# Transposing q and k of the later chunks by the DMA crossbar instead of on TensorE, in a retention layer followed by a gated FFN

## The chip, the cores and the metric

The kernel runs on one core of a Trainium2 chip. The metric is the device time of one execution in microseconds (us). A time "before" and a time "after" are medians of several executions on the same chip. The profiled execution's span, which is from the first to the last instruction that the profile shows, is some 1.7 us shorter than its device time (246.4 us for 248.13), so spans are compared with spans and times with times. Ratios are the mean time of one kernel's fast runs over that of the other's of the same rounds, which is not quite the ratio of the medians quoted. A run counts as slow when it is over 1.5% above the fastest of the same kernel; all others are fast.

## The reference

Two layers. The first is a recurrent attention with a decaying state, for 4 batches, 8 heads, 768 positions and head width 64; the second a gated feed-forward net on its 3072 tokens of width 512.

```
state = gamma[h] * state + outer(k[t], v[t])        # per batch and head
y[t]  = q[t] @ state / sqrt(64)
x     = y as (3072, 512)
out   = (sigmoid(x @ w_gate) * (x @ w_val)) @ w_out  # d_ff = 1536
```

## The kernel before

The positions are cut into chunks of 128 (24 chunks over all batches, numbered g), and the tokens into six tiles t of 512. In a chunk the attention is a few small matmuls: scores of k against q, a mask, the product with v, and a term with the state of the chunks before. For these, q and k must be transposed (64 head dimensions on the partitions). TensorE does this, into PSUM, and ScalarE copies the result to SBUF:

```python
def transposes(g):
    tp = pa.tile([128, 2 * NP, C], BF16, tag="tp", name="tp")
    for i, x in enumerate((kn[g], qn[g])):
        for p in range(NP):                                   # NP = 4 pairs of heads
            nc.tensor.transpose(tp[:, i * NP + p, :], pair(x, p), ident)
    qkT[g] = at.tile([128, 2 * NP, C], BF16, tag="qkT", name="qkT", bufs=3)
    nc.scalar.activation(qkT[g], tp, AX.Copy)

def step_t(g):
    transposes(g)
    scale_v(g, nc.vector if g < 8 else nc.gpsimd)

def step_s(g):
    scores(g)
    masks(g)
```

The feed-forward groups of tile t are interleaved with the attention steps of tile t + 1, and the loads of the chunks after that are issued by GpSimd at the start of the tile. Each engine is given its instructions in program order:

```python
def attention(t):            # nine steps for the four chunks of tile t
    g = 4 * t
    return [lambda: step_t(g), lambda: step_s(g), lambda: step_t(g + 1), lambda: step_y(g, g + 1), ...]

for t in range(NT):
    groups = [lambda n1=n1: up(t, n1) for n1 in range(0 if t else 4, NFF)]   # 12 groups of 8 matmuls
    groups += [lambda sm=sm: down(t, sm) for sm in range(4)]                 # 4 groups of 12, each with an output store by SyncE
    steps = attention(t + 1) if t + 1 < NT else []
    if t + 2 < NT:
        for g in range(4 * t + 8, 4 * t + 12):
            load_chunk(g)                                                    # three DMAs issued by GpSimd
    ...                                                                      # a group, then as many steps as are due
```

Of the kernel before, what the change touches and what calls it, by code (L numbers as in the profile page):

```python
# [10 lines left out]
BF16 = mybir.dt.bfloat16  # L11
# [6 lines left out]
def kernel(  # L18
# [10 lines left out]
    nc = tc.nc  # L29
# [3 lines left out]
    C = 128  # L33
    NCH = S // C
    NP = H // 2
# [8 lines left out]
    ld = ctx.enter_context(tc.tile_pool(name="ld", bufs=12))  # L44
# [5 lines left out]

    NG = B * NCH
    NT = N_TOK // 512
    qn, kn, vf = {}, {}, {}

    def src(x, g):
# [3 lines left out]
    def load_v(g, eng):  # L59
        vf[g] = ld.tile([C, H, D], F32, tag="vf", name="vf", bufs=8)  # L60
        eng.dma_start(out=vf[g], in_=src(v, g))  # L61

    def load_kq(g):
        kn[g] = ld.tile([C, H, D], BF16, tag="kn", name="kn")
        qn[g] = ld.tile([C, H, D], BF16, tag="qn", name="qn")
        nc.gpsimd.dma_start(out=kn[g], in_=src(k, g))  # L66
        nc.gpsimd.dma_start(out=qn[g], in_=src(q, g))  # L67

    def load_chunk(g):
        load_kq(g)  # L70
        load_v(g, nc.gpsimd)
# [55 lines left out]
    xT, vs, qkT, sc, stA, stB, y = {}, {}, {}, {}, {}, {}, {}  # L127
    zps = {}

    def pair(t, p):  # L130
        return t[:, 2 * p:2 * p + 2, :].rearrange("s h d -> s (h d)")
# [4 lines that stand above are left out]
            for p in range(NP):  # L136
                nc.tensor.transpose(tp[:, i * NP + p, :], pair(x, p), ident)  # L137
        qkT[g] = at.tile([128, 2 * NP, C], BF16, tag="qkT", name="qkT", bufs=3)
        nc.scalar.activation(qkT[g], tp, AX.Copy)  # L139

    def scale_v(g, eng):
        vs[g] = ld.tile([C, H, D], BF16, tag="vs", name="vs", bufs=4)
        eng.tensor_tensor(vs[g], vf[g], tabv[:, g % NCH, :].unsqueeze(2).to_broadcast([C, H, D]),  # L143
                          op=ALU.mult)
# [52 lines left out]
        nc.vector.tensor_tensor(xT[g // 4][:, :, col:col + C], y[g], taby[:, :, c * C:(c + 1) * C], op=ALU.mult)  # L197

    def step_t(g):
        transposes(g)  # L200
        scale_v(g, nc.vector if g < 8 else nc.gpsimd)

    def step_s(g):
# [14 lines left out]
    def attention(t):  # L218
        g = 4 * t
        return [lambda: step_t(g), lambda: step_s(g), lambda: step_t(g + 1), lambda: step_y(g, g + 1),  # L220
                lambda: step_t(g + 2), lambda: step_y(g + 1, g + 2), lambda: step_t(g + 3),
                lambda: step_y(g + 2, g + 3), lambda: step_y(g + 3)]
# [4 lines left out]
    def up(t, n1, lo=0, hi=512):  # L227
        if t not in hT:
            hT[t] = ffn.tile([128, NFF, 512], BF16, tag="hT", name="hT", bufs=2)
        ps = []  # L230
        for w in (wg, wv):
            u = pf.tile([128, 512], F32, tag="ff", name="ff")
            for kk in range(KT):
                nc.tensor.matmul(u[:, lo:hi], w[:, kk, n1 * 128:(n1 + 1) * 128], xT[t][:, kk, lo:hi],  # L234
                                 start=(kk == 0), stop=(kk == KT - 1))
            ps.append(u)
        gs = ffn.tile([128, 512], F32, tag="gs", name="gs")
        nc.scalar.activation(gs[:, lo:hi], ps[0][:, lo:hi], AX.Sigmoid)  # L238
        nc.vector.tensor_tensor(hT[t][:, n1, lo:hi], gs[:, lo:hi], ps[1][:, lo:hi], op=ALU.mult)  # L239

    def down(t, sm):
        o = pf.tile([128, 512], F32, tag="ff", name="ff")
        for n1 in range(NFF):
            nc.tensor.matmul(o, hT[t][:, n1, sm * 128:(sm + 1) * 128], wo[:, n1, :],  # L244
                             start=(n1 == 0), stop=(n1 == NFF - 1))
        ob = ffn.tile([128, D_MODEL], F32, tag="ob", name="ob")
        nc.scalar.copy(ob, o)  # L247
        row = t * 512 + sm * 128
        nc.sync.dma_start(out=out[row:row + 128, :], in_=ob)
# [23 lines left out]
    transposes(0)  # L273
    keep_on(8)
    scale_v(0, nc.vector)
    scores(0)
    state(0)
# [3 lines left out]
    make_taby(slice(256, 384))  # L281
    transposes(1)
    scale_v(1, nc.vector)
    inter(0)
    intra(0)
# [41 lines left out]

    for t in range(NT):
        groups = [lambda n1=n1: up(t, n1) for n1 in range(0 if t else 4, NFF)]
        groups += [lambda sm=sm: down(t, sm) for sm in range(4)]  # L330
        steps = attention(t + 1) if t + 1 < NT else []
        if t + 2 < NT:
            for g in range(4 * t + 8, 4 * t + 12):
                load_chunk(g)
        first = 0 if t else 6
        done = 0
        for i, group in enumerate(groups):
            group()
            upto = -(-len(steps) * (i + 1 - first) // (len(groups) - first))
            while done < min(upto, len(steps)):  # L340
                steps[done]()
                done += 1
# [30 lines left out]
```

## Time and profile before

| | before |
|---|---|
| time, median of 3 | 248.32 us (248.23 to 248.34) |
| span of the profiled run | 246.4 us |
| TensorE busy | 234.1 us, 95% |
| next engine (ScalarE) | 106.0 us, 43% |
| tile 2 / 3 / 4, first matmul to first matmul | 37.27 / 37.14 / 37.37 us |
| eight transposes of a chunk on TensorE | 0.445 us |

The page cuts the span into 40 slices of 6.2 us; each digit is the busy share of a slice in tenths (9 is 90% or more), and PEclk is the granted clock of TensorE in tenths. PE is TensorE, PEld its weight loads, DVE VectorE, ACT ScalarE, POOL GpSimd, SP SyncE; SPq or ACTq is the issue of a DMA by that engine, and L153 is line 153 of the kernel. From the kernel before:

```profile
PE   7689998997999999999999999999999999999993
...
PEclk9999999999999999999999999999999999999998
DMA  9999999999999932994012100002100002200022
```

From the fourth slice to the last but one TensorE is busy and at full clock, but for two dips before 62 us. The DMA engines are full in the first 14 slices, and full once more in slices 17 and 18, from about 98 to 111 us: these are the last twelve loads. They begin where tile 2 begins.

### The profile page before, as it was taken

What the parts mean: (1) busy time and instruction counts of PE and PEld (TensorE: products, weight loads), DVE (VectorE), ACT (ScalarE), POOL (GpSimd) and SP (SyncE); (2) the same over time, 40 slices, a digit from 0 to 9 for tenths busy, and PEclk for the clock granted to TensorE, in tenths of its full rate; (3) what the DMA queues carried; (4) which work ended last, traced back from release to release, by engine and by line L of the source; (5) the groups of instructions that cost most, each with busy time, mean ns of one, the idle gap of its engine ahead of it and who ended that gap; (6) DMA issues with size and microseconds to landing.
All of it is one profiled execution on the core that took longest, in us unless ns stands there. A gap on an engine that the chain in (4) does not pass through costs nothing.

```text
span 246.4 us, 4449 instructions
## 1 busy us (share of the span) xinstructions
PE 234.1 (95%) x1816; PEld 123.3 (50%) x1816; DVE 101.5 (41%) x168; ACT 106.0 (43%) x191; POOL 91.5 (37%) x111
## 2 busy tenths in 40 slices
PE   7689998997999999999999999999999999999993
PEld 7565644554455554445554445544445554444441
DVE  2565444563446631246631256541256532234300
ACT  7788333425444431454443444342444542233221
POOL 8986574987999912961111001111000000000000
PEclk9999999999999999999999999999999999999998
DMA  9999999999999932994012100002100002200022
GB/s 146 181 198 196 192 213 203 176 208 232 229 174 127 188 80 84 145 180 61 3 41 78 54 3 3 0 17 92 64 0 3 0 0 88 85 0 3 0 85 85
DMA packets 64212, 24.13 MB, mean 98 GB/s; under 512 B 51969, under 2 KB 59649, under 8 KB 64193
## 3 DMA queue, kind: packets, MB, share of 16 engines
q0 software_dynamic: 57616, 16.78, 62.2%
q1 hardware_dynamic: 5536, 6.82, 8.2%
q10 hardware_dynamic: 1040, 0.26, 0.5%
q8 instruction: 14, 0.23, 0.4%
q14 instruction: 6, 0.04, 0.1%
HBM read 28.31 MB, written 6.29 MB: 140 GB/s over the span
## 4 chain that ended last, share of the span: by engine, by line
PE 91%; ACT 7%; issue 1%; DVE 0%; POOL 0%; POOLq 0%; ACTq 0%
PE ff L234 50%; PE ff L244 26%; PE tp L137 4%; PE sA L153 3%; ACT qkT L139 2%; PE y L189 2%; ACT taby L122 2%; PE z L175 2%; PE y L165 2%; PE ff L254 2%; ACT zbd L183 1%; ACT L307 1%; ACT ob L247 0%; ACT gs L238 0%; DVE xT L197 0%
## 5 line engine op out<-in xcount | busy, mean ns | idle before, releaser
L239 DVE TENSOR_TENSOR hT<-gs,ff 128x512 bf16<-128x512 f32 (+2 forms) x76 | 50.1, 660 | 85.6 <-PE ff L234 81.9
L234 PE MATMUL ff<-xT,wg 128*128 128x512 bf16 (+2 forms) x304 | 74.7, 368 | 1.2 <-DVE xT L197 1.1
L234 PE MATMUL ff<-xT,wv 128*128 128x512 bf16 (+2 forms) x304 | 74.6, 368 | 0.0
L238 ACT ACTIVATE gs<-ff 128x512 f32<-128x512 f32 (+2 forms) x76 | 43.6, 573 | 55.4 <-PE ff L234 55.4
L244 PE MATMUL ff<-wo,hT 128*128 128x512 bf16 x288 | 65.0, 379 | 0.0
L234 PEld LDWEIGHTS <-wv 128*128 128x128 bf16 x304 | 29.3, 98 | 33.2
L244 PEld LDWEIGHTS <-hT 128*128 128x128 bf16 x288 | 27.3, 98 | 32.1
L234 PEld LDWEIGHTS <-wg 128*128 128x128 bf16 x304 | 27.4, 98 | 28.4 <-issue 1.4
L143 POOL TENSOR_TENSOR vs<-vf,tabv 128x512 bf16<-128x512 f32 x16 | 16.6, 1058 | 65.0 <-PE y L189 60.1
L247 ACT COPY ob<-ff 128x512 f32<-128x512 f32 x24 | 14.1, 586 | 54.9 <-PE ff L244 50.5
L139 ACT ACTIVATE qkT<-tp 128x1024 bf16<-128x1024 bf16 x24 | 24.6, 1024 | 13.4 <-PE tp L137 13.3
L197 DVE TENSOR_TENSOR xT<-y,taby 128x512 bf16<-128x512 f32 x24 | 16.4, 684 | 20.6 <-PE y L189 20.6
L158 DVE TENSOR_TENSOR stA<-sA,causal 128x512 bf16<-128x512 f32 x24 | 16.5, 687 | 19.9 <-PE sB L153 19.9
L61 POOL DMA_DIRECT2D vf<-in_v_dram x23 | 21.0, 913 | 5.0 <-issue 2.0
L66 POOL DMA_DIRECT2D kn<-in_k_dram x23 | 21.0, 913 | 3.3 <-DMA wo<-in_moe_w_out_dram 1.7
L67 POOL DMA_DIRECT2D qn<-in_q_dram x23 | 20.6, 897 | 2.6 <-DMA wo<-in_moe_w_out_dram 1.7
L183 ACT CAST zbd<-z 64x256 bf16<-64x256 f32 x40 | 14.7, 367 | 12.1 <-PE z L175 11.8
L159 DVE TENSOR_TENSOR stB<-sB,causal 128x512 bf16<-128x512 f32 x24 | 16.3, 680 | 0.0
L153 PE MATMUL sA<-qkT 64*128 64x128 bf16 x96 | 9.5, 219 | 5.5 <-ACT qkT L139 5.4
L153 PEld LDWEIGHTS <-qkT 64*128 64x128 bf16 x192 | 5.4, 94 | 10.6 <-ACT qkT L139 6.8
L254 PE MATMUL ff<-ident 128*128 128x128 bf16 x104 | 9.0, 252 | 1.6 <-POOL ident masks.py:199 1.6
L189 PE MATMUL y<-stA,vs 128*64 128x128 bf16 x96 | 9.9, 222 | 0.0
(36 smaller groups left out, 123.1 us busy)
## 6 DMA issues: line engine op xcount, KB each, us to landing
out_dram<-ob SPq DMA_DIRECT2D x24, 256.0 KB, 2.0
vf<-in_v_dram POOLq DMA_DIRECT2D x23, 256.0 KB, 7.2
kn<-in_k_dram POOLq DMA_DIRECT2D x23, 128.0 KB, 7.2
qn<-in_q_dram POOLq DMA_DIRECT2D x23, 128.0 KB, 7.1
wg<-in_moe_w_gate_dram POOLq DMA_DIRECT2D x6, 256.0 KB, 8.7
wv<-in_moe_w_val_dram POOLq DMA_DIRECT2D x6, 256.0 KB, 9.2
wo<-in_moe_w_out_dram POOLq DMA_DIRECT2D x4, 384.0 KB, 10.7
qf<-in_q_dram ACTq DMA_DIRECT2D x1, 256.0 KB, 4.5
```

Source lines behind the costliest of these rows:

```text
L61: eng.dma_start(out=vf[g], in_=src(v, g))
L66: nc.gpsimd.dma_start(out=kn[g], in_=src(k, g))
L67: nc.gpsimd.dma_start(out=qn[g], in_=src(q, g))
L139: nc.scalar.activation(qkT[g], tp, AX.Copy)
L143: eng.tensor_tensor(vs[g], vf[g], tabv[:, g % NCH, :].unsqueeze(2).to_broadcast([C, H, D]), op=ALU.mult)
L153: nc.tensor.matmul(sc[g][i][:, p, :], t[half, p, :], t[half, NP + p, :], start=True, stop=True)
L158: nc.vector.tensor_tensor(stA[g], sc[g][0], causal4, op=ALU.mult)
L183: nc.scalar.copy(zbd[g % 2][half, :, half], zps[b][half])
L234: nc.tensor.matmul(u[:, lo:hi], w[:, kk, n1 * 128:(n1 + 1) * 128], xT[t][:, kk, lo:hi], start=(kk == 0), stop=(kk == KT - 1))
L238: nc.scalar.activation(gs[:, lo:hi], ps[0][:, lo:hi], AX.Sigmoid)
L239: nc.vector.tensor_tensor(hT[t][:, n1, lo:hi], gs[:, lo:hi], ps[1][:, lo:hi], op=ALU.mult)
L244: nc.tensor.matmul(o, hT[t][:, n1, sm * 128:(sm + 1) * 128], wo[:, n1, :], start=(n1 == 0), stop=(n1 == NFF - 1))
```

## The change

The intent is to take the transposes of chunks 12 to 23 off the bounding engine and leave them to the DMA crossbar, which goes from SBUF to SBUF without PSUM and ScalarE.

```diff
+    XBAR = 12
...
+    def xbar(g):
+        qkT[g] = ld.tile([128, 2 * NP, C], BF16, tag="qkX", name="qkX", bufs=8)
+        for i, x in enumerate((kn[g], qn[g])):
+            nc.sync.dma_start_transpose(out=qkT[g][:, i * NP:(i + 1) * NP, :],
+                                        in_=x.rearrange("s h d -> s (h d)"))
...
     def step_t(g):
-        transposes(g)
+        if g < XBAR:
+            transposes(g)
         scale_v(g, nc.vector if g < 8 else nc.gpsimd)
...
         if t + 2 < NT:
             for g in range(4 * t + 8, 4 * t + 12):
                 load_chunk(g)
+        for g in range(4 * t + 4, 4 * t + 8):
+            if XBAR <= g < NG:
+                xbar(g)
```

## The prediction

> **What bounds the kernel now.** I read first the page's busy shares and its row of granted clock, then the chain of work that ended last in order of time, then the busy times by stretch, with a stretch for each 512-token tile, and last the timeline and the DMA landings around the place where the new transfers start. The page says that TensorE is busy nearly all the span and that nothing else comes near it:
>
> ```profile
> PE 234.1 (95%) x1816; PEld 123.3 (50%) x1816; DVE 101.5 (41%) x168; ACT 106.0 (43%) x191; POOL 91.5 (37%) x111
> ```
>
> Columns are busy us, share and instruction count. Busy time of pipelined matmuls overlaps, so I do not use it as work, only as absence of gaps. The busy times by stretch show where there are none; I cut at the first matmul of tiles 2, 3, 4 and 5, which the chain gives:
>
> ```profile
> 99.65:136.92 37.27, 37.27 (x286) 18.80 (x284) 15.62 (x24) 16.05 (x28) 13.16 (x15) 1.00 0.65 86
> 136.92:174.06 37.14, 37.14 (x278) 18.68 (x276) 15.62 (x24) 15.26 (x26) 4.17 (x4) 1.00 0.08 30
> 174.06:211.43 37.37, 37.37 (x282) 18.99 (x280) 15.64 (x24) 15.37 (x26) 0.00 (x0) 1.00 0.08 29
> ```
>
> After the length come busy us of PE, PEld, DVE, ACT and POOL, then clock, DMA share, GB/s. In the three tiles that the change touches, TensorE is busy for the whole length at full clock. So in this stage an instruction taken off TensorE is worth its start-to-start time, and a wait put on TensorE costs its whole length. ScalarE at 16 of 37 us is far from binding. The chain of waits in order of time (start, length, what) then shows what one tile looks like, here the start of tile 2 and of tile 3:
>
> ```profile
> 99.65 1.73 PE ff L234 x8
> 101.38 0.45 PE tp L137 x8
> 101.82 1.73 PE ff L234 x8
> 103.55 0.16 PE sA L153
> ...
> 136.92 1.73 PE ff L234 x8
> 138.65 0.45 PE tp L137 x8
> 139.09 1.73 PE ff L234 x8
> 140.82 0.16 PE sA L153
> ```
>
> The eight transposes of a chunk take 0.44 to 0.45 us of TensorE's stream, not 8 x 219 ns. And the first scores of a tile, which read the transposed q and k, come only 3.9 us after the tile starts: two "up" groups and one set of transposes. That second fact decides the case. The change is described as one tile ahead, but in program order the transfers of chunks 4t+4 to 4t+7 are issued at the start of tile t, and these chunks' attention steps are run inside tile t. The lead of the first chunk is two groups, not a tile.
>
> **What the Trainium skill says.** "TensorE: Matmul & The Clock Gate", Part 1 (The HAM clock gate), measures 55.6 ns from start to start of warm matmuls with N = 128, and says that an idle window of about 3.4 us can put the clock back to half. The trace agrees with the first (0.445 / 8 = 55.6 ns); no long gap exists in it to show the second. "VectorE: DVE Perf Modes", The three transpose paths, gives 1309 ns for one 128x128 bf16 transpose by the DMA crossbar against 390 ns on TensorE; the trace has no crossbar transpose. "DMA: Bandwidth & Descriptors", Latency and other measured facts, gives a transpose rate of 261 GB/s in one kernel; not in this trace either. The same page, Queues, rings and completion order, says that a DMA engine goes round its queues packet by packet, so that loads issued by GpSimd and transfers issued by SyncE share it. The trace agrees: the same 256 KB output store lands in 2.0 us in quiet and in 4.2 us when loads run (below).
>
> **The change, part by part.**
>
> Removed from TensorE: 12 chunks (12 to 23, four in each of tiles 2, 3, 4) x 0.445 us = 5.34 us, all of it on the path. This is the most that can be won: 248.32 - 5.34 = 243.0, 2.15%.
>
> Removed from ScalarE: 12 evictions of 1024 ns, 12.3 us. None of that is on the path: in these tiles TensorE never waits for one.
>
> Added: 24 transfers of 128 KB, SBUF to SBUF, on SyncE's queue, eight at the start of each of three tiles. SyncE is in order, and the last output store of the tile before stands ahead of them. It waits for the copy of the last "down" result. In the timeline (start, length, what) of tiles 2 and 3:
>
> ```profile
> 100.34 0.33 SPq L249 DMA_DIRECT2D out_dram<-ob  x1
> 137.61 0.33 SPq L249 DMA_DIRECT2D out_dram<-ob  x1
> ```
>
> So the first transpose can be issued at 100.67 and 137.94. With their own transposes gone, the scores are due at 103.55 - 0.44 = 103.1 and 140.82 - 0.44 = 140.4. Both k and q must land in 2.4 us, behind a 256 KB store on the same queue. Tile 4 is the same (store at 174.76, scores due at 177.5).
>
> Quiet tiles (3 and 4). The store issued at 137.61 lands 2.0 us later, at 139.6; I take 0.5 us of this as its acknowledgement, so that its data end near 139.1. Then 256 KB of k and q at 261 GB/s take 1.0 us, and landing another 0.5: 140.6, 0.2 us late. If the rate is half that for transfers this small, or if SyncE needs nearer 1 us than 0.33 us to issue one, it is 1.2 to 1.5 us late. I take 0.8 us for each of the two tiles, an estimate from these two ends.
>
> Tile 2 is not quiet. GpSimd runs ahead: blocked until 97.0 by buffers of the scaled v, it then issues the twelve loads of chunks 20 to 23 from 98.0 to 109, just as the transposes begin. The stretches of DMA and the landings of DMAs issued from 100 to 101 us:
>
> ```profile
> 98.00:113.00 15.00, 15.00 (x109) 7.35 (x108) 6.19 (x10) 6.73 (x11) 11.42 (x14) 1.00 1.49 171
> 113.00:120.00 7.00, 7.00 (x63) 3.75 (x62) 4.33 (x8) 3.54 (x7) 1.29 (x2) 1.00 0.03 6
> 137.60:145.00 7.40, 7.40 (x54) 3.78 (x53) 3.44 (x6) 3.30 (x5) 0.00 (x0) 1.00 0.10 37
> ```
>
> ```profile
> vf<-in_v_dram POOLq DMA_DIRECT2D x1, 256.0 KB, 6.9
> out_dram<-ob SPq DMA_DIRECT2D x1, 256.0 KB, 4.2
> ```
>
> A DMA share over 1 means that the engines hold more than one packet at a time: they are full until 113, then empty. The store ahead of the transposes lands at 104.5, already after the scores are due; data done near 104.0. With half the engines' turns, 256 KB at 130 GB/s take 2.0 us, with landing 106.5: TensorE waits 3.4 us. A wait of this length may also cost a stretch at half clock.
>
> Later chunks of a tile are due 7 to 25 us after the first, and their transfers run meanwhile; even at 3 us apiece they come in time in a quiet tile. Buffers don't bind: eight destination buffers hold two tiles of chunks, and a chunk's buffer is read last two tiles before it is wanted again.
>
> Sum: 248.32 - 5.34 + 3.4 + 2 x 0.8 = 248.0 us.
>
> **Rivals.**
>
> First, everything is hidden: the crossbar lands k and q in under 2.4 us even behind the store. For it speaks that SBUF to SBUF needs no HBM access and that the store's own data are 1 us of traffic. Against it speaks tile 2, where a plain store already lands too late. With tiles 3 and 4 free and tile 2 at 2.5 us: 245.5. Hidden in all three: 243.0.
>
> Second, the crossbar itself becomes the bound. If one 128x512 transfer cost four times the 1309 ns of one 128x128 (5.2 us, an estimate from the skill's figure), a tile would need 8 x 5.2 = 42 us against 35.4 us of matmul work, each first chunk would be 9 to 10 us late, and later ones too: three tiles would go to over 45 us, about 270 in all. Against it: 1309 ns for 32 KB looks like a latency, and 261 GB/s for a real kernel contradicts it.
>
> Third, the middle with more loss: contention in tile 2 costs 6 us and the gap brings half clock for some us, quiet tiles lose 2 us each: 248.3 - 5.3 + 6 + 2 + 4 = 255.
>
> Fourth, unburdening ScalarE or the PSUM bank of the transposes helps elsewhere. Nothing in the three tiles waits for them, so I give this nothing.
>
> **Range and chances.** The gain is sure to some hundredths of a us and the loss is open, from 2.5 us to some 10 us, most likely about 5. This puts the middle at 248.0 and 8 chances in 10 between 244.5 and 252.5. Faster by over 2% (under 243.35) needs under 0.4 us of waits in all, which tile 2's loads all but exclude: 0.05. Slower by over 2% (over 253.3) needs 10 us of waits: 0.14. Within 2%: 0.81.
>
> **What would show it.** In the changed profile: no transposes after 93 us; tiles 2 to 4 would have 35.4 us of matmuls each, and one gap on TensorE in each, ahead of the first scores, released by the DMA that writes the q and k tile, about 3.4 us in tile 2 and about 0.8 us in tiles 3 and 4. The store ahead of the transposes would land at times like before. Wrong would be: gaps ahead of the second to fourth chunk's scores (then the rate of the crossbar is the matter), no gap at all, a lower granted clock in tile 2 for long, or gaps of equal size in all three tiles (then issue or latency, not the loads, set them).

## More of the kernel before

The page's list of DMA queues (packets, MB, share of 16 engines) will be needed later:

```profile
q0 software_dynamic: 57616, 16.78, 62.2%
q1 hardware_dynamic: 5536, 6.82, 8.2%
```

Queue q0 has the loads that GpSimd issues, q1 what SyncE issues.

## The result, and the profile after

The time after is 256.01 us (255.13 to 256.66, 4 runs) against 248.30 us; the ratio is 1.0309, 95% interval 1.0272 to 1.0345. The change is slower by 3%, outside the predicted range. (Line numbers are shifted by the added lines: the "up" matmuls are at L242, the "down" matmuls at L252, the scores at L160.) The page of the kernel after:

```profile
PE 228.4 (90%) x1694; PEld 118.1 (47%) x1720; DVE 101.6 (40%) x168; ACT 95.1 (38%) x179; POOL 91.6 (36%) x111
...
PE   6679998988999999249999979999979999999993
...
PEclk9999999999999999959999999999999999999999
DMA  9999999999999916999601264002253002200022
```

TensorE lost work as intended, and its row now has three holes, at slices 17 to 18, 24 and 30: the beginnings of tiles 2, 3 and 4. The first hole is deep and wide, and the clock drops in it. The busy DMA stretch of slices 17 to 19 is longer than before. The waits of the kernel after name the cause (who waited, for what: us in total, times, longest):

```profile
PE sA L160 <- DMA qkX<-qn: 10.7, 3, 7.8
```

There are just three waits, one ahead of the first scores of each tile, for the landing of the transposed q. Second to fourth chunks of a tile cause none. The timeline at the starts of tile 2 and tile 3 (start, length, what, idle time before it) shows both sizes:

```profile
100.85 1.36 SPq L145 DMA_TRANSPOSE qkX<-kn  x1
102.31 1.28 SPq L145 DMA_TRANSPOSE qkX<-qn  x1
...
110.98 0.26 PE L160 MATMUL sA<-qkX 64*128 64x128 bf16 x1 [7.80 <-DMA qkX<-qn]
...
145.52 1.23 SPq L145 DMA_TRANSPOSE qkX<-kn  x1
...
146.84 1.22 SPq L145 DMA_TRANSPOSE qkX<-qn  x1
...
149.32 0.21 PE L160 MATMUL sA<-qkX 64*128 64x128 bf16 x1 [1.46 <-DMA qkX<-qn]
```

Tile 2's wait is 7.80 us, tile 3's 1.46 us, and tile 4 has the rest of the 10.7, 1.44 us. In the quiet tile 3 SyncE is occupied for 1.22 us with each transpose (a plain store takes it 0.33 us), and q is there 2.44 us after its own start (landing at 149.28). In tile 2 it is there 8.63 us after its start (landing at 110.94).

The busy times by stretch around tile 2's hole (length, busy us of PE, PEld, DVE, ACT, POOL, then clock, DMA share, GB/s) show what followed the hole:

```profile
103.00:111.00 8.00, 0.20 (x3) 0.12 (x4) 0.69 (x1) 0.00 (x0) 5.73 (x7) 0.75 1.76 159
111.00:113.00 2.00, 2.00 (x12) 0.91 (x12) 1.29 (x2) 0.00 (x0) 0.00 (x0) 0.50 2.24 170
113.00:115.00 2.00, 2.00 (x8) 0.79 (x7) 0.36 (x1) 0.60 (x1) 0.00 (x0) 0.80 1.18 115
115.00:117.00 2.00, 2.00 (x11) 0.91 (x10) 0.96 (x2) 0.60 (x1) 0.00 (x0) 1.00 1.77 66
```

The clock fell to half at 107.0 us, 3.8 us after TensorE ran dry. The matmuls after the hole start at half clock, at 110.98, and are at full clock again from 113.8 us, 2.8 us later.

The balance on spans: 246.4 - 5.34 (transposes gone) + 10.7 (waits) + 1.3 (half clock, measured below) = 253.1, against a span of 253.4 us.

My theory after this comparison had three parts. In tile 2 the transposes share the DMA engines with the twelve loads and are late for that. In the quiet tiles they are late because two transposes cost SyncE 1.3 us each and the lead is 2.4 us. And both are a matter of lead alone, as nothing else suffers. The rivals: tile 2's transposes are slow by themselves, behind the store and each other; each tile pays alike; transposes slow something else too.

### The profile page after: what moved, and what is told of

Read it like the earlier page. It is cut to its first block, busy times and chain, and to the rows that moved or that the text cites. A ratio compares the mean times of both kernels' runs of the same rounds, so it can differ in the third digit from the quotient of the medians.

```text
span 253.4 us, 4271 instructions
## 1 busy us (share of the span) xinstructions
PE 228.4 (90%) x1694; PEld 118.1 (47%) x1720; DVE 101.6 (40%) x168; ACT 95.1 (38%) x179; POOL 91.6 (36%) x111
## 3 DMA queue, kind: packets, MB, share of 16 engines
q1 hardware_dynamic: 18592, 9.97, 17.7%
## 4 chain that ended last, share of the span: by engine, by line
PE 79%; ACT 9%; DMA 7%; issue 2%; SPq 1%; POOL 1%; DVE 0%; ACTq 0%
PE ff L242 45%; PE ff L252 23%; DMA qkX<-qn 5%; PE sA L160 3%; ACT taby L123 3%; ACT qkT L140 2%; PE y L196 2%; PE z L182 2%; PE y L172 2%; PE tp L138 2%; DMA qn<-in_q_dram 1%; ACT ob L255 1%; ACT zbd L190 1%; SPq L145 1%; ACT L315 1%
## 5 line engine op out<-in xcount | busy, mean ns | idle before, releaser
L242 PE MATMUL ff<-xT,wg 128*128 128x512 bf16 (+2 forms) x293 | 74.4, 371 | 1.7 <-DVE xT L204 1.1
L242 PE MATMUL ff<-xT,wv 128*128 128x512 bf16 (+2 forms) x296 | 73.8, 369 | 0.4
L252 PE MATMUL ff<-wo,hT 128*128 128x512 bf16 x281 | 64.3, 379 | 0.5 <-issue 0.2
L242 PEld LDWEIGHTS <-wv 128*128 128x128 bf16 x304 | 29.4, 98 | 33.7 <-issue 1.0
L242 PEld LDWEIGHTS <-wg 128*128 128x128 bf16 x304 | 28.0, 98 | 31.7 <-issue 2.2
L252 PEld LDWEIGHTS <-hT 128*128 128x128 bf16 x288 | 27.3, 98 | 32.1
L160 PE MATMUL sA<-qkX 64*128 64x128 bf16 x48 | 4.9, 224 | 10.7 <-DMA qkX<-qn 10.7
L140 ACT ACTIVATE qkT<-tp 128x1024 bf16<-128x1024 bf16 x12 | 12.3, 1023 | 4.8 <-PE tp L138 4.8
L160 PE MATMUL sA<-qkT 64*128 64x128 bf16 x48 | 4.7, 219 | 5.5 <-ACT qkT L140 5.4
```

Of the source, the lines that this page charges most:

```text
L160: nc.tensor.matmul(sc[g][i][:, p, :], t[half, p, :], t[half, NP + p, :], start=True, stop=True)
L242: nc.tensor.matmul(u[:, lo:hi], w[:, kk, n1 * 128:(n1 + 1) * 128], xT[t][:, kk, lo:hi], start=(kk == 0), stop=(kk == KT - 1))
L252: nc.tensor.matmul(o, hT[t][:, n1, sm * 128:(sm + 1) * 128], wo[:, n1, :], start=(n1 == 0), stop=(n1 == NFF - 1))
```

## The experiments

All results were correct. The diffs are against the changed kernel unless said otherwise.

**Only the quiet tiles.**

```diff
-    XBAR = 12
+    XBAR = 16
```

> Chunks 12 to 15 keep their TensorE transposes; only chunks 16 to 23 go through the crossbar, so only the two quiet tiles (3 and 4) are changed. My theory (each quiet tile gains 4 x 0.445 us and loses one wait of 1.46 us, the loss is tile 2's loads): 248.3 - 3.56 + 2.92 = 247.7 us, no drop of the granted clock. Rival (every tile pays alike, a third of the 7.7 us lost): 253.4 us.

Measured: 248.14 us (247.90 to 248.38), before 248.25, ratio 0.9995 (0.9980 to 1.0010). The waits:

```profile
PE sA L160 <- DMA qkX<-qn: 3.0, 2, 1.6
```

Two waits of 1.5 us each, as in the changed kernel's quiet tiles, and hardly any gain is left: a quiet tile wins 1.78 us and loses 1.5. The rival, that every tile pays alike, is out. The time is some 0.4 us above the expectation, which the interval nearly covers; the traces show most of it before anything was changed, as the first scores of tile 2 come at 103.89 us here and at 103.55 in the kernel before.

**The loads moved away from tile 2's transposes.**

```diff
             for g in range(4 * t + 8, 4 * t + 12):
-                load_chunk(g)
+                if t != 3:
+                    load_chunk(g)
...
+            if t == 3 and i == 0:          # after tile 3's first step; GpSimd gets there at 114 us
+                for g in range(20, 24):
+                    load_chunk(g)
```

> All twelve chunks through the crossbar, but the loads of chunks 20 to 23 come after tile 2's first step in GpSimd's order, so that they start when tile 2's first transposes have landed. Contention theory: tile 2's wait ahead of the first scores falls from 7.8 us to the 1.46 us of the quiet tiles, no clock drop, 248.3 - 5.34 + 3 x 1.46 = 247.4 us. Rival (tile 2's transposes are slow by themselves, behind the store and each other): the wait stays near 7.8 us, time 255 to 256 us.

(The expectation says "after tile 2's first step". The edit puts the loads after tile 3's first step in program order, which GpSimd reaches while TensorE is in tile 2.) Measured: 247.70 us (247.65 to 247.80), ratio 0.9977 (0.9960 to 0.9993), clock 1.00.

```profile
PE sA L160 <- DMA qkX<-qn: 4.5, 3, 1.6
```

Three waits of 1.5 us. With the loads gone from this stretch, tile 2 is a quiet tile: its first q lands 2.43 us after its issue in place of 8.63. The store ahead of it and the six transposes behind it are still there, so they are not the cause. This is the experiment that decides that the loads are; how they slow the transposes it does not show.

**Keeping the clock up in the hole.**

```diff
     def step_s(g):
+        if g == 12:
+            keep_on(125)      # 125 idle matmuls of 128 columns
         scores(g)
```

> The changed kernel with 125 idle matmuls of 128 columns (6.95 us at full clock) put on TensorE where it waits 7.8 us in tile 2. If the half clock after the gap costs 1.4 us, as the stretches suggest, this comes out 1.4 us below the changed kernel, near 254.6 us with the clock at 1.00 throughout, although TensorE has more to do. Rival (the clock after the gap costs nothing that the wait does not hide): the same as the changed kernel, 256 us, or more.

Measured: 255.24 us (254.93 to 255.94), ratio to before 1.0285. The clock stayed up, but the ranges of this and of the changed kernel overlap and they had not run in the same rounds. The trace is clearer. In the chain of waits, the first scores of tile 2 and the next ones, in the changed kernel:

```profile
110.98 0.26 PE sA L160
...
119.72 0.16 PE sA L160
```

and with the idle matmuls:

```profile
112.13 0.21 PE sA L160
...
119.54 0.16 PE sA L160
```

The same instructions took 8.74 us at the lowered clock and 7.41 us at full clock, a difference of 1.33 us. But here q had landed 1.1 us later than in the changed kernel, which made the total undecided, so both were run again side by side with more rounds:

> The changed kernel once more, beside the next run on the same chip: 256 us, wait of 7 to 9 us in tile 2, half clock after it.

> The idle matmuls in the wait once more. From the first scores of tile 2 to the next ones it took 7.41 us here and 8.74 us in the changed kernel, so 1.3 us lower than the changed kernel of the same rounds if the crossbar's landing is the same in both (254.7 us). Rival (what is won on the clock is lost by a later landing, because TensorE's reads slow the transfers): no difference, and a landing of q about 1 us later again.

Measured: the changed kernel 256.33 us (255.69 to 257.02), with idle matmuls 254.89 us (254.74 to 255.19). The difference is 1.44 us and the ranges are apart; in these runs q landed at 112.10 and 111.87 us, so the rival, that the landing eats the gain, is out. From the first scores of tile 2 to the next it took 8.77 and 7.42 us, 1.35 apart. The half clock after the hole costs 1.3 to 1.4 us.

**Issued one tile earlier.**

```diff
-        for g in range(4 * t + 4, 4 * t + 8):
+        for g in range(4 * t + 8, 4 * t + 12):
             if XBAR <= g < NG:
                 xbar(g)
```

> The transfers are issued one tile earlier, so that those of the chunks used in tile t run in tile t - 1. Lead theory (all of the loss is that the first chunk's lead is 2.4 us): no wait on TensorE for the crossbar, all 5.34 us gained, 243.0 us (242.8 to 243.6). Rival (the transposes slow something else too, TensorE's reads of SBUF or the loads that are wanted in time): more than 244.5 us with waits elsewhere.

Measured: 242.78 us (242.76 to 243.32), ratio 0.9784 (0.9770 to 0.9799): the gain is 5.47 us of the 5.34 expected. TensorE waits for no transpose any more; GpSimd does once, for 1.9 us, without cost. The two quieter tiles of this kernel by stretch (columns as before):

```profile
136.00:171.00 35.00, 35.00 (x244) 16.73 (x243) 15.63 (x24) 11.44 (x22) 4.17 (x4) 1.00 0.28 61
171.00:206.00 35.00, 35.00 (x247) 16.96 (x246) 15.63 (x24) 11.27 (x22) 0.00 (x0) 1.00 0.08 31
```

The transposes themselves were slower than ever here: those of tile 1 landed up to 15.6 us after their start, as they lay among the loads. It did not matter, since they had a tile of 35 us. The rival is half right: transposes do slow the loads (in the changed kernel the loads' queue moved 1.04 MB from 101 to 111 us, in the kernel before 1.62 MB), but TensorE waits for none of them. This version beats both kernels.

**Ahead of the last store of the tile before**, on the kernel with the later loads:

```diff
-        for g in range(4 * t + 4, 4 * t + 8):
-            if XBAR <= g < NG:
-                xbar(g)
...
+            if i == 14:                    # before the last "down" group and its store
+                for g in range(4 * t + 8, 4 * t + 12):
+                    if XBAR <= g < NG:
+                        xbar(g)
```

> The kernel with the later loads (waits of 1.5 us in each of three tiles, 247.7 us), with the eight transposes put ahead of the last output store of the tile before in SyncE's order, which starts them some 3 us earlier. Lead theory: 3 us more lead is more than the 1.5 us that lack, no wait, all 5.34 us: 243.0 us; the last store of each tile is 8 to 10 us late and nothing waits for it. Rival (quiet tiles lose by something other than the lead): stays at 247 us or more.

Measured: 242.97 us (242.85 to 243.03), ratio 0.9781 (0.9767 to 0.9796), no wait of TensorE for a transpose. The first transpose of tile 2 starts at 97.72 us, where it started at 101.06 with the later loads: some 3 us more lead are enough for a tile without loads.

**The first chunk of each tile left on TensorE.**

```diff
-        if g < XBAR:
+        if g < XBAR or g % 4 == 0:
             transposes(g)
...
-            if XBAR <= g < NG:
+            if XBAR <= g < NG and g % 4:
                 xbar(g)
```

> Of each four chunks the first keeps its TensorE transposes, the other three go through the crossbar at the start of the tile as in the change, with tile 2's loads where they were. If only the first chunk's lead is too short: 9 x 0.445 = 4.0 us gained and no wait, 244.3 us; in tile 2 the second chunk's q, second in the queue, would land near 111 us where it is due near 111, so 0 to 1 us of wait there is possible. Rival (later chunks are late too, because loads and transposes share the engines): several us of wait in tile 2, above 247 us.

Measured: three runs of 244.72 to 245.50 us, ratio of these 0.9869 (0.9853 to 0.9886); but the fourth, which was the profiled one, took 1330.76 us with every matmul slow. So it was run again:

> The kernel with the first chunk of each tile on TensorE once more, because the run that was profiled last time took 1330 us, with every matmul slow, and says nothing of the waits. Times near 245.2 us again. That is 0.9 us above 244.3, so a wait of about 0.9 us ahead of the second chunk's scores in tile 2, where the loads run, and none in tiles 3 and 4. Rival: no wait, and the 0.9 us lie elsewhere.

Measured: three runs of 244.78 to 245.87 us, ratio 0.9878 (0.9857 to 0.9898), and again the profiled first run was slow, 521.85 us. The page's row of granted clock shows when it turned:

```profile
PEclk9999999999999921111111111111111111111111
```

The slices are 13 us here, so all up to 182 us ran at full clock, and in the stretch from 95 to 182 us the only wait for a transpose is this one, in tile 2:

```profile
PE sA L160 <- DMA qkX<-qn: 0.8, 1, 0.8
```

So it is as expected: chunk 13, which is now first in the queue, is late by 0.8 us among the loads, and no later chunk of tiles 2 and 3 is late. Tile 4 lies for the most part in the slowed stretch and says nothing. The cause of the two slow executions is not known. They came on two chips, both times in the first execution of this kernel in a job and in no later one, and nothing here explains them.

**One transfer for k and q**, on the kernel with the later loads:

```diff
-        kn[g] = ld.tile([C, H, D], BF16, tag="kn", name="kn")
-        qn[g] = ld.tile([C, H, D], BF16, tag="qn", name="qn")
+        kq[g] = ld.tile([C, 2, H, D], BF16, tag="kq", name="kq")
+        kn[g], qn[g] = kq[g][:, 0], kq[g][:, 1]
...
-        for i, x in enumerate((kn[g], qn[g])):
-            nc.sync.dma_start_transpose(out=qkT[g][:, i * NP:(i + 1) * NP, :],
-                                        in_=x.rearrange("s h d -> s (h d)"))
+        nc.sync.dma_start_transpose(out=qkT[g][:, :, :], in_=kq[g].rearrange("s x h d -> s (x h d)"))
```

> The kernel with the later loads, with k and q of a chunk side by side in one buffer and one transpose of 128 x 1024 in place of two of 128 x 512. If SyncE's 1.22 us is a cost per instruction, the pair lands near 2.5 us after it is issued in place of 3.8, the quiet wait falls from 1.5 to about 0.2 us: 243.8 us. If it grows with the size, issue takes 2.4 us, and the wait stays near 1.4 us: 247.5 us.

Measured: 246.25 us (246.18 to 246.59), ratio 0.9917 (0.9900 to 0.9933), between the two expectations. The issue of a transpose (min/median/max ns) with 128 x 1024 elements, and the waits:

```profile
L144 SPq DMA_TRANSPOSE qkX<-kq x12: 1231/1275/2339, 101.1 to 178.5; - x12
...
PE sA L158 <- DMA qkX<-kq: 3.2, 3, 1.1
```

Twice the size is issued in nearly the same time, 1.28 us for 1.22: SyncE's cost is one per instruction. But landing takes longer after that: in a quiet tile the pair landed 3.30 us after it was issued, of which 2.0 after the issue had ended, where a single one had 1.2. So a pair in one instruction is there 0.4 us sooner than in two, not 1.3, and the wait is 1.07 us. My expectation had left out that the bytes take time too.

**Chunks 8 to 11 as well, one tile ahead.** The kernel issued one tile earlier, with XBAR = 8:

> One tile ahead, and chunks 8 to 11 as well: their transfers are issued at the start of tile 0, in a stretch in which the loads keep the DMA engines full and chunk 8 itself has hardly landed. If the DMA engines were no limit: 16 x 0.445 = 7.1 us gained, 241.2 us. My theory: the transfers wait for loads that land only from 60 us on and then share full engines, chunk 8 is due at about 66 us, so TensorE waits 5 us or more in tile 1 and the whole is above 244 us, worse than starting at chunk 12.

Measured: 257.22 us (255.56 to 259.70, of which the highest counts as slow and is not in the ratio), ratio 1.0333 (1.0296 to 1.0370). It is slower as expected, but not for the reason given. Chunk 8's q landed at 62.8 us, in time. The wait is another:

```profile
PE ff L242 <- ACT ob L255: 12.8, 1, 12.8
```

TensorE waited for ScalarE's copy of a "down" result; that had no free buffer, because the stores which free them stood in SyncE's queue behind transposes, and those waited for loads: the first of tile 0's four stores left at 69.0 us, where before it left at 48.3.

**The stores moved to ScalarE's queue**, in that kernel:

```diff
-        nc.sync.dma_start(out=out[row:row + 128, :], in_=ob)
+        nc.scalar.dma_start(out=out[row:row + 128, :], in_=ob)
```

> One tile ahead from chunk 8 on, as in the run that was slower, with the output stores issued from ScalarE's queue instead of SyncE's. There TensorE waited 12.8 us for the copy of a result whose buffers were held by stores queued behind transposes that waited for loads. If that order is the whole cause, the wait goes and 16 x 0.445 = 7.1 us are gained: 241.2 us (241 to 242.5). Rival (chunk 8 comes too late by itself): a wait for the crossbar in tile 1 of some us, above 244 us.

Measured: 274.71 us (273.32 to 277.57, the highest again counted as slow), ratio 1.1051 (1.1001 to 1.1102). Much worse, and again the expectation failed. The waits on ScalarE for transposes:

```profile
ACT zbd L190 <- DMA qkX<-kn: 22.0, 1, 22.0
...
ACT ob L255 <- DMA qkX<-qn: 7.5, 1, 7.5
...
ACT qkT L140 <- DMA qkX<-kn: 5.7, 1, 5.7
```

ScalarE stood still for 22 us in front of a store, which waited for a transpose whose data it does not touch; the state copy behind it came late, and TensorE with it. The compiled program shows why (instruction order and the semaphores waited for, names shortened; not part of the trace):

```
L145 DmaTransposeAnt qkX<-qn   SyncE    [waits DMAHW2, DMASW7]
L257 DMACopy out_dram<-ob      ScalarE  [waits DMAHW7, Activation]
L257 DMACopy out_dram<-ob      ScalarE  [waits DMAHW2, Activation]
```

In this program eight completion semaphores (DMAHW0 to 7) are dealt out in turn to the DMAs of both queues, in program order, and each DMA first waits until the last user of its semaphore has landed. The last user of DMAHW7 before the first of these stores is the transpose of chunk 10's k, that of DMAHW2 before the second chunk 11's q. So a store on the other queue was still tied to the transposes ahead of it. This is how the program was compiled; no run shows that the chip demands it. The three waits, each ahead of a store, add up to 35.2 us of ScalarE, near the 33 us above the expectation, but how far they alone account for it was not tested.

## Why the prediction was wrong, point by point

The mechanism was the predicted one: the lead of the first chunk is two groups, TensorE waits there once in each tile, three waits and no others, longest in tile 2 for the sake of the loads. The sizes were wrong, all to the same side.

- *Removed from TensorE, 5.34 us.* Right. Issued with enough lead, the change gains 5.47 us (242.78 against 248.25) and in another form 5.40 us.
- *ScalarE's evictions worth nothing.* Right: the gain has no room for more.
- *Lead of 2.4 us.* Right: SyncE reached the first transpose at 100.85 us, and TensorE was ready for the scores near 103.2.
- *Quiet tiles, 0.8 us each.* Too small: 1.46 and 1.44, which lie in the bad end of 1.2 to 1.5 that I had named. I took the middle between a SyncE that needs 0.33 us and one that needs 1 us to issue a transpose. It needs 1.22, and the two one after the other are most of the 3.8 us from first issue to landing. The rate was the smaller part: in the run with one transfer, 128 KB more landed 0.8 us later after the end of the issue. The 0.5 us taken as acknowledgement has no number of a trace behind it.
- *Tile 2, 3.4 us.* This is the step that failed: "With half the engines' turns, 256 KB at 130 GB/s take 2.0 us". The store ahead landed at 105.02, close to the 104.5 of before. But k then landed at 106.94 and q at 110.94, 6 us after the store and not 2.0. From the landing of the store to that of q the DMA view of the changed kernel has (packets, MB, share of 16 engines):

```profile
q0 software_dynamic: 2554, 0.57, 130.3%
q1 hardware_dynamic: 1034, 0.25, 41.5%
```

So in these 5.92 us the transposes' queue moved 0.25 MB, which is 42 GB/s, a third of the 130 of the prediction. Both of its factors were too high: the transposes got 29% of the packets and not half, and the two queues together moved 139 GB/s and not 261. A transpose is cut into many packets, 544 each (the 24 added 18592 - 5536 = 13056 to queue q1), so the 1034 are nearly the pair's 1088. Why the loads had 2.5 packets to one of the transposes is not shown. What the runs do show is that without the loads the wait is 1.5 us.
- *Half clock after the wait.* I named it as possible and left it out of the sum. The wait of 7.8 us made it real, and it costs 1.3 to 1.4 us. "TensorE: Matmul & The Clock Gate", Part 1, says that idling for about 3.4 us lowers the clock to half. The runs agree: it fell 3.8 us into the wait, and waits of 1.5 us did not lower it (1.00 at both quiet tiles' starts).
- *Sum.* Predicted loss 3.4 + 1.6 = 5.0 us; measured 7.8 + 2.9 + 1.3 = 12.0 us. The third rival had nearly this number (6 + 4 + 2, in other proportions), and I kept it outside the range.

What the profile of the changed kernel was to show came as told but for the sizes; of the signs of being wrong one came too, the lower clock in tile 2, for 6.8 us. The lesson for the range is that the gain had a ceiling in the trace of before and the two waits had only a floor: no row of it measured a crossbar transpose, alone or among loads, so the upper end needed more room than the lower.

## What to carry to other kernels

Moving work from the bounding engine to the DMA engines pays in full if the transfer is issued so early that even a slowed one is in time; judge the lead from the place in program order where it is issued to the instruction that needs it, not from the loop index. Here the same transfers, with one range shifted by four chunks, turned 3% slower into 2.2% faster. And when a DMA queue works in order, ask what stands behind a transfer that may wait: stores that free buffers can stop the bounding engine from there.

## What the Trainium skill lacked or had wrong

- "DMA: Bandwidth & Descriptors", SWDGE vs HWDGE vs iDMA, calls the hardware descriptor path quicker to set up than the software one. The page has no measured issue time of a crossbar transpose on this chip (only cycle counts for unnamed earlier chips, for other sizes). Here SyncE is occupied 1.22 us for 128 x 512 and 1.28 us for 128 x 1024 elements of two bytes, against 0.33 us for a plain store, and a quiet one lands 2.4 or 3.3 us after its start.
- The same page, Latency and other measured facts, gives 261 GB/s for transposes. In the quiet tile 3 most of the eight of 128 KB start 1.31 us apart, which is 131072 B / 1.31 us = 100 GB/s, bounded by the issue; the page does not say from which size its rate holds.
- The same page, Queues, rings and completion order, has each engine go round its queues packet by packet, as the prediction cites, and does not say what share transposes then get beside loads. Here the profile counts 1034 packets to 2554, not half.
- "VectorE: DVE Perf Modes", The three transpose paths, has 1309 ns for one 128x128 transpose by the crossbar and nothing of one among loads. Here a 128 x 512 transpose took 2.4 us in quiet and 6 to 15.6 us among loads, whose landings in turn grew from 7 to up to 19 us.
- "TensorE: Matmul & The Clock Gate", Part 1, says that the clock is either half or full, apart from a limit of 13/16 that takes three busy cores; it also warns that the records can't always be trusted and that the clock has been seen stuck at a quarter for over 50 us. Two executions on one busy core went below that: in one the granted clock was 0.16 from about 185 us to the end, and it took 521.85 us; in the other, of 1330.76 us, matmuls came about six times as far apart as usual (116 in 100 us) while the clock was recorded as 1.0. The warning fits the second; no cause is known.
- No page says that DMAs of both hardware queues can be tied together by a small number of completion semaphores, as in the program compiled here. Eight of them made ScalarE wait 22 us ahead of a store, behind a transpose that SyncE had issued.
